# Last transform of a long convolution taken for two token blocks at once, with the MLP's inner units split six and eight

## The chip, the core and the metric

The kernel runs on one core of one Trainium2 chip, as one launch. The metric is the device time of that launch in microseconds; the number quoted for a kernel is the median of its runs. A profiled execution gives the span of the core (first to last recorded instruction), the busy time of each engine, and the waits between engines. The engines are TensorE (PE; its weight loads are listed as PEld), VectorE (DVE), ScalarE (ACT), GpSimd (POOL) and SyncE (SP). In this kernel nearly all DMA transfers are issued by SP, one after the other, in program order.

## The reference

One block of a network with adaptive layer norm: a state-space convolution over 2048 tokens and 448 channels, and behind it an MLP that mixes tokens (not channels), with 1792 inner units.

```python
def _A_ref(u, log_A_real, A_imag, C_real, C_imag, log_dt, D_skip):
    L = u.shape[1]
    ...
    K = 2.0 * jnp.einsum("dn,dnl->dl", C, P).real
    L2 = 2 * L
    u_t = u.transpose(0, 2, 1)
    Kf = jnp.fft.rfft(K, L2)
    Uf = jnp.fft.rfft(u_t, L2)
    y = jnp.fft.irfft(Uf * Kf[None, :, :], L2)[:, :, :L]
    return y.transpose(0, 2, 1) + u * D_skip[None, None, :]

def _B_ref(x, w1, b1, w2, b2):
    h = _layernorm(x, axis=-1)                     # (B, S, D)
    u = jnp.einsum("bsd,sf->bdf", h, w1) + b1      # (B, D, F)
    u = _gelu(u)
    y = jnp.einsum("bdf,fs->bds", u, w2) + b2      # (B, D, S)
    return y.transpose(0, 2, 1)

h = _layernorm(x, axis=-1) * (1 + ca) + sa
x = x + ga * _A_ref(h, ...)
h = _layernorm(x, axis=-1) * (1 + cb) + sb
x = x + gb * _B_ref(h, ...)
```

## The kernel before

**The convolution.** It is a Fourier transform of length 4096 written as small matrix products in two levels (32 by 64). The last level of the inverse transform brings 32 frequencies, each with a real and an imaginary part, back to tokens. Its input is a scratch tensor in device memory, `v_d`, with 32 rows `k` of 128 positions; a position is (part `c` of 2, half `h` of 2, half `g` of 2, row `r` of 16). Token number 64 n + 32 g + 16 h + r is row `r` of halves `g`, `h` and block number n. So the 2048 tokens fall into 16 blocks, one for each `r`, of 128 tokens each.

**From the transform to the MLP.** Each block `r` passes through four stages. `ln_load` reads its 128 x 896 slice `vt` of `v_d`; every other call also reads, with `x_pair`, the input rows `x` of two neighbouring blocks into a tile `xt`. `ln_y` does the transform on TensorE: two products of 128 x 64 weights (`ft`, in which half of the entries are zero, since `h` is kept apart by a block diagonal) into the two halves of the single PSUM tile `y`; then VectorE adds `y` to `xt` with the row sum, and ScalarE takes the square sum. `ln_mod` normalizes and scales, with a second row sum and square sum; `ln_out` normalizes again (the MLP's own layer norm) and splits the block into a rounded part `h3h` and a remainder `h3l`. `mlp1` then multiplies the block with seven 128-column pieces of `w1`: three products a piece (`whi` by `h3h`, `whi` by `h3l`, `wlo` by `h3h`), accumulated in seven PSUM tiles `acc` over all 16 blocks.

**The two passes.** PSUM has eight banks; seven hold `acc`, one holds `y`. So the 1792 inner units are done as two passes of seven 128-unit pieces: the first pass runs together with the transform and the norms, the second reads the finished `h3h`, `h3l` again. Behind each pass `gelu` empties the `acc` tiles. Then the MLP's second layer runs: 16 output blocks `o`, each with 42 products.

**The weights.** `WeightStream` loads `w1` and `w2` through three tiles `w`, 448 KB each; ScalarE rounds `w` to `whi`, VectorE takes the remainder `wlo`. `begin` does the first, `rest` the second and then issues the next load. Four `whi`, `wlo` pairs are kept ahead.

**What sets the order.** The norm phase is a loop of steps t = -3 to 15 whose instructions run on PE, ACT and DVE exactly as written; in step t the program does `ln_out` of block t+1, `ln_y` of block t+3, the load of block t+7, `ln_mod` of block t+2, the weight split, and then `mlp1` of block t. SP's order is also as written from the last loads of the convolution on (`manual_schedule`). `vt` has four buffers, `w` three, `y` one. Ahead of it the convolution's last pieces run: `u` loads, products on VectorE and GpSimd (`zx`, `zy`, `z`), inverse products `vv` on TensorE, copies `vt` on ScalarE and stores to `v_d`. All of `v_d` has to be stored before the first `vt` can be read.

Of the kernel before, what the change touches and what calls it, by code (L numbers as in the profile page):

```python
# [11 lines left out]
F32 = mybir.dt.float32  # L12
# [27 lines left out]
def dft_tables():  # L40
# [75 lines left out]
    ft = np.zeros((32, 2, 2, 32, 2))  # L116
# [32 lines left out]

def token_rows(a):  # L150

    return a.rearrange("(n g h r) d -> r g n h d", g=2, h=2, r=16)


def token_pair(a, r, g):

    rows = a.rearrange("(n g h r) d -> g n h (r d)", g=2, h=2, r=16)
    return rows[g, :, :, r * D : (r + 2) * D]


class WeightStream:
# [12 lines left out]
    def load(self):  # L174
# [3 lines left out]
        w = self.pool.tile([P, 896], F32, tag="w", name="w", bufs=3)  # L178
        if n < 32:
            fh, r = divmod(n, 16)  # L180
            for g in range(2):
                self.nc.sync.dma_start(w[64 * g : 64 * g + 64], self.w1[r, g, :, :, fh * 896 : (fh + 1) * 896])
        else:
            t, kh = divmod(n - 32, 2)
            self.nc.sync.dma_start(
                w.rearrange("p (k s) -> p k s", k=7), self.w2[:, 7 * kh : 7 * kh + 7, t * P : (t + 1) * P]
            )
# [6 lines left out]
    def begin(self, most):  # L194
# [5 lines left out]
        hi = self.pool.tile([P, 896], F32R, tag="whi", name="whi")  # L200
        lo = self.pool.tile([P, 896], F32R, tag="wlo", name="wlo")
# [15 lines left out]
def tile_adaln_s4d_mixer(ctx, tc, i, out):  # L217
# [14 lines left out]
    ft = cp.tile([P, 64], F32, name="ft")  # L232
# [5 lines left out]
    with ExitStack() as es:  # L238
# [894 lines left out]
        py = e3.enter_context(tc.tile_pool(name="py", bufs=1, space=PSUM, side="right"))  # L1133
        xts = [xs.tile([P, 2, D], F32, name=f"xt{r}") for r in range(8)]

        def x_pair(r):
            for g in range(2):
                nc.sync.dma_start(
                    xts[r // 2][64 * g : 64 * g + 64].rearrange("p r d -> p (r d)"), token_pair(x, r, g)
                )  # L1140
# [4 lines left out]
        for m in range(NP, 2 * NP + 2, 2):  # L1145
# [31 lines left out]
    with ExitStack() as es:  # L1177
# [7 lines left out]
        uh = [up.tile([P, 7, D], F32R, name="uh0"), None]  # L1185
        ul = [up.tile([P, 7, D], F32R, name="ul0"), None]
        v_v = v_d.rearrange("k (ch g r) d -> r (k ch) g d", ch=4, g=2)

        def mlp1(acc, n, f0=0, f1=7):
            fh, r = divmod(n, 16)  # L1190
            hi, lo = wst.parts[n]
            if f1 == 7:
# [9 lines left out]
        def ln_load(r):  # L1202
# [161 lines left out]
```

## Time and profile before

| | before |
|---|---|
| median of 3 runs | 719.15 us (715.73 to 719.76) |
| the profiled execution's own time | 720.78 us |
| its span | 719.0 us |
| busy PE, DVE, ACT, POOL | 632.4, 453.2, 438.7, 273.6 us |
| HBM traffic | 84.64 MB read, 34.87 MB written |

The median and the profiled execution differ by 1.63 us, and 1.78 us of the execution lie outside the span. Times in views of the trace count from the span's start. A row of the timeline gives start, duration, engine, line and operation; what stands in brackets is the engine's idle time just before and what ended it. Matmuls are pipelined: one of 448 columns shows a duration of 0.36 us, but in a dense stream the next starts 0.20 us after it, so counts times start distances give the time, not counts times durations. A float32 product (the transform) is shown as two instructions, a rounded one (`fp32r`, the MLP) as one.

### The profile page before, as it was taken

Reading aid. Unit: us, or ns where it says so; the run is one execution under the profiler, and the core shown is the slowest. Engines: PE = TensorE matmul, PEld = TensorE weight load, DVE = VectorE, ACT = ScalarE, POOL = GpSimd, SP = SyncE. Lnnn points to the kernel's source line nnn. Section 1 sums busy time; section 2 is a strip of 40 time slices with the busy share of each in tenths; the row PEclk is TensorE's granted clock in tenths of the full one; section 3 lists DMA queues with packets and bytes.
Section 4 is the critical chain, followed back from the end, with each engine's and each line's share of the span. In section 5 each row is a group of like instructions: output and inputs, shape, how many; then the busy total and the mean of one; then the engine's idle time right before and its main releaser. Section 6 shows DMA issues by size and latency. Waiting matters only on the chain. (4 is left out here: it accounts for less than half of the span.)

```text
span 719.0 us, 18288 instructions
## 1 busy us (share of the span) xinstructions
PE 632.4 (88%) x7204; PEld 456.4 (63%) x7204; DVE 453.2 (63%) x875; ACT 438.7 (61%) x876; POOL 273.6 (38%) x328
## 2 busy tenths in 40 slices
PE   0659889979989888799888949999999999999997
PEld 0335335434535556566565617778999999999996
DVE  7469879679778668586684548778622263334441
ACT  5847588887987789989883549787522242222220
POOL 6486437528737787878785600000000000000000
PEclk9868857988998889999899959999999999999999
DMA  7795464266888635535236989974585436655540
GB/s 169 207 191 131 162 192 138 113 229 179 244 227 248 204 92 133 149 100 154 70 102 181 285 245 266 239 195 113 174 231 146 148 109 172 173 155 154 156 139 26
DMA packets 101635, 121.19 MB, mean 169 GB/s; under 512 B 13066, under 2 KB 87422, under 8 KB 101422
## 3 DMA queue, kind: packets, MB, share of 16 engines
q1 hardware_dynamic: 100014, 113.16, 55.2%
q0 software_dynamic: 1536, 6.87, 4.4%
q8 instruction: 57, 0.93, 0.6%
q14 instruction: 28, 0.23, 0.1%
HBM read 84.64 MB, written 34.87 MB: 166 GB/s over the span
## 5 line engine op out<-in xcount | busy, mean ns | idle before, releaser
L202 ACT CAST whi<-w 128x896 fp32r<-128x896 f32 x64 | 59.7, 938 | 131.4 <-PE o L1331 84.7
L651 POOL TENSOR_TENSOR G<-mag,gs 128x512 f32<-128x512 f32 x56 | 71.9, 1284 | 92.4 <-ACT gs L647 92.1
L211 DVE TENSOR_TENSOR wlo<-w,whi 128x896 fp32r<-128x896 f32 x64 | 68.0, 1087 | 40.3 <-ACT whi L202 31.0
L603 PE MATMUL xg<-tab,lph 64*128 64x512 f32 x112 | 68.8, 617 | 25.9 <-ACT xg L649 8.0
L1196 PE MATMUL acc<-h3h,whi 128*128 128x448 f32 x224 | 83.3, 372 | 0.1
L1197 PE MATMUL acc<-h3l,whi 128*128 128x448 f32 x224 | 81.9, 366 | 0.0
L1331 PE MATMUL o<-ul,whi 128*128 128x448 f32 x224 | 81.3, 363 | 0.0
L1330 PE MATMUL o<-uh,whi 128*128 128x448 f32 x224 | 81.2, 362 | 0.0
L1198 PE MATMUL acc<-h3h,wlo 128*128 128x448 f32 x224 | 80.9, 361 | 0.0
L1332 PE MATMUL o<-uh,wlo 128*128 128x448 f32 x224 | 80.6, 360 | 0.0
L678 PEld LDWEIGHTS kg<-E,G 128*32 128x32 f32 x3584 | 59.8, 119 | 32.3 <-issue 16.4
L603 PE MATMUL xe<-tab,lph 64*128 64x512 f32 x112 | 67.8, 609 | 12.2 <-ACT gs L648 10.2
L678 PE MATMUL kg<-E,G 128*32 128x64 f32 x3584 | 69.8, 235 | 2.2 <-issue 1.5
L652 POOL TENSOR_TENSOR G<-mag,gs 128x512 f32<-128x512 f32 x56 | 71.7, 1280 | 0.0
L653 DVE TENSOR_TENSOR E<-m,xe 128x512 f32<-128x512 f32 x56 | 38.3, 683 | 40.8 <-ACT xe L646 31.8
L632 POOL TENSOR_TENSOR m<-mag,w 128x512 f32<-128x512 f32 x56 | 59.9, 1070 | 6.0 <-DVE E L657 1.5
L1334 DVE SCALAR_TENSOR_TENSOR y<-o,b,mod 128x448 f32<-128x448 f32 x16 | 10.9, 684 | 80.3 <-PE o L1332 80.3
L644 ACT ACTIVATE ab<-xe 128x512 f32<-128x512 f32 x56 | 33.7, 601 | 30.3 <-PE xe L603 16.1
L1196 PEld LDWEIGHTS acc<-h3h,whi 128*128 128x128 f32 x224 | 42.3, 189 | 13.8 <-ACT h L1252 6.3
L603 PE MATMUL xe<-tab,lex 64*128 64x512 f32 x56 | 31.7, 575 | 18.8 <-POOL dsk L468 17.2
L614 ACT ACTIVATE mag<-xe 128x512 f32<-128x512 f32 x56 | 35.5, 634 | 19.7 <-PE xg L603 14.0
L603 PEld LDWEIGHTS xg<-tab,lph 64*128 64x128 f32 x112 | 24.3, 217 | 36.3 <-issue 10.3
(229 smaller groups left out, 1486.1 us busy)
## 6 DMA issues: line engine op xcount, KB each, us to landing
w<-in_B_w_dram SPq DMA_DIRECT2D x64, 224.0 KB
w<-in_B_w_dram SPq DMA_DIRECT2D x32, 448.0 KB
yu_d<-yt SPq DMA_DIRECT2D x16, 448.0 KB
yi<-yu_d SPq DMA_DIRECT2D x32, 224.0 KB
us_d<-uo SPq DMA_DIRECT2D x16, 448.0 KB
u<-us_d SPq DMA_DIRECT2D x32, 224.0 KB
v_d<-vt SPq DMA_DIRECT2D x32, 224.0 KB
vt<-v_d SPq DMA_DIRECT2D x16, 448.0 KB
```

Source lines behind the costliest of these rows:

```text
L211: eng.tensor_tensor(lo, w, hi.bitcast(F32), ALU.subtract)
L603: T.matmul(out[k], lhs[r], rhs[r], start=start, stop=stop)
L632: G.tensor_tensor(m2, me, w[:, :, None].to_broadcast([P, GD, 32]), ALU.mult)
L651: G.tensor_tensor(Gt[:, 1], mg_, v32(sg), ALU.mult)
L652: G.tensor_tensor(Gt[:, 0], mg_, v32(cg_), ALU.mult)
L678: T.matmul(kgs[g][32 * q : 32 * q + 32, m], Gt[:, c, d], E[:, c, d], start=h == 0 and c == 0 and m == 0, stop=h == 1 and c == 1, skip_grou ...
L1196: nc.tensor.matmul(acc[f], hi[:, fs], h3h[:, r], start=r == 0, stop=False)
L1197: nc.tensor.matmul(acc[f], hi[:, fs], h3l[:, r], start=False, stop=False)
L1198: nc.tensor.matmul(acc[f], lo[:, fs], h3h[:, r], start=False, stop=r == 15)
L1330: nc.tensor.matmul(o, hi[:, ks], uh[kh][:, k], start=kh == 0 and k == 0, stop=False)
L1331: nc.tensor.matmul(o, hi[:, ks], ul[kh][:, k], start=False, stop=False)
L1332: nc.tensor.matmul(o, lo[:, ks], uh[kh][:, k], start=False, stop=kh == 1 and k == 6)
```

## The change

The transform takes two blocks at once, `r` and `r + 8`. `ft` becomes 128 x 32: the same 64 x 32 matrix twice, once for each `h`. `vt` is loaded with `h` in the two halves of the partitions (two transfers a block instead of one), so that a block needs four products of 64 x 32 weights, (`h`, `g`), and a pair of blocks eight. Their row half is `h`, and their 32 output columns are `2 g + place`, where `place` is `h` for the first block of a pair and `1 - h` for the second. Thus the eight lie on eight different parts of the array, and the two blocks of a pair write two PSUM tiles `y`.

Two `y` tiles take two banks, so `acc` has six in the first pass, and the 14 pieces of inner units are done as six and eight. The second pass takes the two banks of `y` for its first two pieces. The weight tiles have room for 1024 columns and hold 768 or 1024. The tokens of a block are now stored in four groups of 32 partitions: loads of `w1`, of `x` and the store of the sum are four transfers of 32 partitions where there were two of 64.

The blocks run in the order 0, 8, 1, 9, ...; two tiles of `x` rows are needed from the start, and their loads (`x_pair(0)`, `x_pair(8)`) stand inside the convolution's last pieces. Before, that place had `x_pair(0)` alone, later, and `x_pair(2)` and `x_pair(4)` stood between the first `vt` loads.

```diff
-    ft = np.zeros((32, 2, 2, 32, 2))
+    ft = np.zeros((2, 32, 2, 32))
...
     for h in range(2):
-        ft[:, 0, h, :, h] = f0
-        ft[:, 1, h, :, h] = f1
-    t["FT"] = ft.reshape(P, 64)
+        ft[h, :, 0] = f0
+        ft[h, :, 1] = f1
+    t["FT"] = ft.reshape(P, 32)
...
+def block(b):
+    return 8 * (b % 2) + b // 2
+
+def place(r, c):
+    return c ^ (r >= 8)
+
 def token_rows(a):
-    return a.rearrange("(n g h r) d -> r g n h d", g=2, h=2, r=16)
+    return a.rearrange("(n j r) d -> r j n d", j=4, r=16)
...
+NF = (6, 8)
...
         if n < 32:
             fh, r = divmod(n, 16)
-            for g in range(2):
-                self.nc.sync.dma_start(w[64 * g : 64 * g + 64], self.w1[r, g, :, :, fh * 896 : (fh + 1) * 896])
+            r, cols = block(r), slice(768 * fh, 768 + 1024 * fh)
+            w = w[:, 0 : P * NF[fh]]
+            for c in range(4):
+                self.nc.sync.dma_start(w[32 * c : 32 * c + 32], self.w1[r, place(r, c), :, cols])
...
+            if m == 2 * NP - 6:
+                x_pair(0)
             if m == 2 * NP - 4:
-                x_pair(0)
+                x_pair(8)
...
-        pacc = es.enter_context(tc.tile_pool(name="pacc", bufs=7, space=PSUM))
+        pacc = es.enter_context(tc.tile_pool(name="pacc", bufs=6, space=PSUM))
+        pys.append(e3.enter_context(tc.tile_pool(name="py2", bufs=1, space=PSUM, side="right")))
...
-        v_v = v_d.rearrange("k (ch g r) d -> r (k ch) g d", ch=4, g=2)
+        v_v = v_d.rearrange("k (c h g r) d -> r h k c g d", c=2, h=2, g=2)
...
-        def ln_load(r):
-            vts[r] = rot.tile([P, 2, D], F32, tag="vt", name="vt", bufs=4)
-            nc.sync.dma_start(vts[r], v_v[r])
-            if r % 2 and 1 < r < 15:
-                x_pair(r + 1)
+        def ln_load(b):
+            vts[b] = rot.tile([P, 2, D], F32, tag="vt", name="vt", bufs=4)
+            for h in range(2):
+                nc.sync.dma_start(vts[b][64 * h : 64 * h + 64], v_v[block(b), h])
+            if b > 3 and b % 4 < 2:
+                x_pair(block(b))
...
+        def ln_pair(b):
+            for i in (b, b + 1):
+                ys[i] = pys[i % 2].tile([P, D], F32, tag="y", name="y")
+                vt = vts.pop(i)
+                for h in range(2):
+                    k = slice(64 * h, 64 * h + 64)
+                    for g in range(2):
+                        c = 2 * g + place(block(i), h)
+                        nc.tensor.matmul(ys[i][32 * c : 32 * c + 32], ft[k], vt[k, g], start=True, stop=True)
...
         def ln_y(r):
-            y = py.tile([P, D], F32, tag="y", name="y")
-            vt = vts.pop(r)
-            for g in range(2):
-                nc.tensor.matmul(y[64 * g : 64 * g + 64], ft, vt[:, g], start=True, stop=True)
...
         for r in range(4):
             ln_load(r)
-            if r == 1:
-                x_pair(2)
         wst.load()
...
+            if t in (-3, -1):
+                ln_pair(t + 3)
...
+            if t % 2 and 0 < t < 13:
+                ln_pair(t + 3)
             if t in (-3, -1) or 0 < t < 13:
                 ln_y(t + 3)()
...
         gelu(acc, 0)
-        acc = [pacc.tile([P, D], F32, tag="acc", name="acc") for _ in range(7)]
+        more = es.enter_context(tc.tile_pool(name="more", bufs=2, space=PSUM))
+        acc = [(pacc if f > 1 else more).tile([P, D], F32, tag="acc", name="acc") for f in range(8)]
```

Two places of the order show it. On PE, the rows from the convolution's last inverse products (`vv`) to the first MLP products, before:

```order
L798 MATMUL vv<-z,bt 128x224 x2
L1224 MATMUL y<-vt,ft 64x448 x6
L1196 MATMUL acc<-h3h,whi 128x448
L1197 MATMUL acc<-h3l,whi 128x448
L1198 MATMUL acc<-h3h,wlo 128x448
```

and in the changed kernel:

```order
L815 MATMUL vv<-z,bt 128x224 x2
L1252 MATMUL y<-vt,ft 32x448 x16
L1217 MATMUL acc<-h3h,whi 128x448
L1218 MATMUL acc<-h3l,whi 128x448
L1219 MATMUL acc<-h3h,wlo 128x448
```

Three blocks' transforms of two products each stood ahead of the first MLP product; now four blocks' of four products each do. Later, two transform products stood between one block's 21 MLP products and the next; now eight stand between 36 and 36.

On SP, the last transfers of the convolution (`u` is its last load, `v_d` its stores) and the first of the norm phase, before:

```order
L806 DMA v_d<-vt 128x2x224 x2
L182 DMA w<-in_B_w_dram 64x1x896 x2
L741 DMA u<-us_d 128x448
L806 DMA v_d<-vt 128x2x224 x2
L1138 DMA xt_6073<-in_A_u_dram 64x1x896 x2
L806 DMA v_d<-vt 128x2x224 x4
L1204 DMA vt<-v_d 128x2x448 x2
```

and in the changed kernel:

```order
L823 DMA v_d<-vt 128x2x224 x2
L197 DMA w<-in_B_w_dram 32x768 x4
L1155 DMA xt_6073<-in_A_u_dram 32x896 x4
L758 DMA u<-us_d 128x448
L823 DMA v_d<-vt 128x2x224 x2
L1155 DMA xt_6077<-in_A_u_dram 32x896 x4
L823 DMA v_d<-vt 128x2x224 x4
L1226 DMA vt<-v_d 64x2x448 x8
```

The last `u` load had two transfers between it and the `v_d` stores ahead of it, and now has eight; the first `vt` loads are eight in a row, four blocks' worth.

More of the change, by code (lines that the diff above doesn't have):

```diff
@@ L199, in begin @@
         w = self.raw.pop(n)
[L200 to L201 removed]
+        m = w.shape[-1]
+        hi = self.pool.tile([P, 1024], F32R, tag="whi", name="whi")[:, 0:m]
+        lo = self.pool.tile([P, 1024], F32R, tag="wlo", name="wlo")[:, 0:m]
         self.nc.scalar.copy(hi, w)
```

62 lines of the change are left out of this document (34 added, 28 removed).

## The prediction

> **What bounds the kernel now.** The windows come first: which engine is full, and where. Columns: length of the window, then busy time of PE, PEld, DVE, ACT, POOL with instruction counts, the granted clock, the share of the DMA engines and GB/s.
>
> ```profile
> 395.00:413.00 18.00, 16.70 (x156) 12.28 (x152) 10.83 (x20) 9.17 (x41) 12.39 (x20) 1.00 0.94 284
> 424.00:466.00 42.00, 40.04 (x173) 27.93 (x174) 32.69 (x102) 33.49 (x76) 0.00 (x0) 0.91 1.05 259
> 450.00:492.50 42.50, 42.50 (x202) 32.51 (x201) 32.45 (x98) 33.41 (x72) 0.00 (x0) 1.00 0.81 201
> 512.60:714.00 201.40, 201.40 (x1009) 188.66 (x1007) 77.35 (x99) 48.57 (x55) 0.00 (x0) 1.00 0.52 148
> ```
>
> From 437 us on PE never stops: in the norm phase, and in the 201.4 us of second pass and second layer, 1008 products at 0.20 us each. There only fewer or cheaper PE instructions save time. Next I read one period of the norm phase, from the chain of waits (start, duration, engine, tile):
>
> ```profile
> 457.57 0.90 PE y L1224 x4
> 458.48 0.41 PE acc L1196
> 462.88 0.90 PE y L1224 x4
> ```
>
> The period is 5.31 us. Twenty-one MLP products at 0.20 us are 4.20, so one block's transform costs PE 1.11 us. The same period on DVE and ACT, from the timeline:
>
> ```profile
> 473.17 0.16 DVE L1244 TENSOR_TENSOR mean<-mean,rs 128x1 f32<-128x1 f32 x1
> 474.44 0.62 DVE L1227 SCALAR_TENSOR_TENSOR xt<-xt,y 128x448 f32<-128x448 f32 x1 [1.12 <-PE y L1224]
> 475.30 0.67 ACT L1216 ACTIVATE sq<-xt,mean 128x448 f32<-128x448 f32 x1 [0.56 <-DVE mean L1214]
> 476.87 0.67 ACT L1216 ACTIVATE sq<-h,mean 128x448 f32<-128x448 f32 x1 [0.48 <-DVE mean L1214]
> 477.28 1.08 DVE L211 TENSOR_TENSOR wlo<-w,whi 128x896 fp32r<-128x896 f32 x1
> 477.86 0.93 ACT L202 CAST whi<-w 128x896 fp32r<-128x896 f32 x1
> ```
>
> DVE waits 1.12 us a period for `y` and nothing else, ACT 0.56 + 0.48 for DVE. So DVE needs 5.31 - 1.12 = 4.19 us a block and ACT 4.27: the reserve under PE is only about 1 us. Last the entrance to the phase, where PE is idle, from the timeline and (the row of `v_d` without a line) the chain of waits:
>
> ```profile
> 404.79 0.95 SPq L806 DMA_DIRECT2D v_d<-vt  x2
> 405.79 1.18 SPq L182 DMA_DIRECT2D w<-in_B_w_dram  x2
> 407.07 0.53 SPq L741 DMA_DIRECT2D u<-us_d  x1
> 411.23 0.62 DVE L781 TENSOR_TENSOR zx<-kx,u 128x448 f32<-128x448 f32 x1 [1.91 <-DMA u<-us_d]
> 415.23 2.07 DMA v_d<-vt
> 417.48 1.23 SPq L1204 DMA_DIRECT2D vt<-v_d  x2
> 421.52 1.76 PE L1224 MATMUL y<-vt,ft 128*64 128x448 f32 x4 [6.99 <-DMA vt<-v_d]
> 423.33 0.62 DVE L1227 SCALAR_TENSOR_TENSOR xt<-xt,y 128x448 f32<-128x448 f32 x1 [3.66 <-PE y L1224]
> 434.13 0.17 DVE L1243 RECIPROCAL rs<-rs 128x1 f32<-128x1 f32 x1 [1.16 <-ACT rs L1217]
> 436.70 0.62 DVE L1254 TENSOR_TENSOR h3l<-h,h3h 128x448 fp32r<-128x448 f32 x1
> 437.07 0.47 PE L1196 MATMUL acc<-h3h,whi 128*128 128x448 f32 x1
> 441.35 0.62 DVE L1254 TENSOR_TENSOR h3l<-h,h3h 128x448 fp32r<-128x448 f32 x1
> 512.46 0.36 PE L1196 MATMUL acc<-h3h,whi 128*128 128x448 f32 x1
> ```
>
> This is one chain: the last `u` load, the last piece of the convolution, its store, the first `vt`, then DVE and ACT in turn up to the remainder `h3l` of block 1 (437.3), when block 1's MLP products begin (437.07). What makes `u` or `vt` late there shifts all that follows. The last row is the start of the second pass (the first pass's last product begins 0.2 us before): 75.4 us after 437.07.
>
> **The change, part by part. The transform of a pair.** What does it cost PE? Rows of the transform, of a full-array float32 product of the same length, and of 64 x 64 products on four parts of the array (line views: least/median/largest ns; timeline):
>
> ```profile
> L1224 PE MATMUL y<-vt,ft x64: 539/590/1009, 421.5 to 495.1; 128*64 128x448 f32 x64
> L557 PE MATMUL pu<-yi,s x64: 539/539/1114, 165.5 to 231.9; 128*128 128x448 f32 x64
> 457.50 0.97 PE L1224 MATMUL y<-vt,ft 128*64 128x448 f32 x4
> 381.75 1.16 PE L716 MATMUL y<-wc,ks 64*64 64x64 f32 x62 [0.22 <-ACT vt L804]
> ```
>
> An instruction takes 0.54 us at any width, yet four of the transform are through in 0.97: the two column halves run side by side, and only the two instructions of one half follow each other. With eight parts the same 0.97 holds for a pair, plus the issue of 12 more instructions. L716 issues 62 in 1.16 us, 0.019 each: 0.23 us. Pair: 1.11 + 0.23 = 1.34 us instead of 2.22. Bounds: 1.11 (issue hidden) and 2.22 (only four parts at once). I take 1.34, since L716 is the nearest row with both row and column parts. The Trainium skill, "TensorE: Matmul & The Clock Gate", section "Measured speedup vs the span model", gives about 4 ns for each further tile; by it the pair would cost about 1.16 us and the sum below would be 0.9 us lower. L716's 19 ns, for short products, does not agree with that figure.
>
> **The first pass.** From block 1's products to the second pass: before, 15 blocks x 21 x 0.20 = 63.0 and eleven transforms x 1.11 = 12.2, together 75.2 (75.4 measured). After, 15 x 18 x 0.20 = 54.0 and five pairs x 1.34 = 6.7: 60.7. **-14.7 us.** The sixth pair lies ahead of block 1's products, as the first did, in a wait for `h3l`.
>
> **The second pass** gets eight pieces: 16 x 3 x 0.20 = **+9.6 us** on a full PE. The two passes and layers hold the same 1344 products; the three of block 0 that leave the first pass save nothing, as PE waits there anyway. At the change of passes PE has no gap today, so the two extra banks win nothing; `gelu` of the second pass's eight pieces lies beside the first six pieces of the second layer (3.6 us).
>
> **DVE and ACT.** Their weight splits shrink by 128/896 in the first pass, 0.14 and 0.13 us: 4.05 and 4.14 us a block, against PE's (36 x 0.20 + 1.34)/2 = 4.27. PE stays the bound by 0.13 us, but not at the start: `h3l` of block 2 ends at 441.97 today, 4.9 us after block 1's products begin, and PE, with 3.6 us of work, is there 0.8 us early (its first product of block 2 does not need `h3l`). **+0.8 us**; between 0.4 and 1.2, and nothing more later, as from block 3 on the pairs put PE behind again.
>
> **SP's queue.** Rows of issue cost:
>
> ```profile
> L182 SPq DMA_DIRECT2D w<-in_B_w_dram x64: 528/578/1782, 382.4 to 552.9; - x64
> L1204 SPq DMA_DIRECT2D vt<-v_d x16: 562/563/613, 417.5 to 479.7; - x16
> L741 SPq DMA_DIRECT2D u<-us_d x32: 319/334/1531, 240.7 to 407.1; - x32
> L589 SPq DMA_DIRECT2D lph<-pars x27: 302/381/2071, 27.2 to 344.2; - x27
> 398.02 0.88 SPq L806 DMA_DIRECT2D v_d<-vt  x2
> ```
>
> Two blocks issue 8 `w`, 4 `vt` and on average 4 `x` transfers, where 4, 2 and 2 stood. Transfers of plain rows (L741, L589, L806) take 0.32 to 0.38, with the gap 0.44 to 0.46; today's `w`, whose 64 partitions are gathered with two strides, 0.58. The new `w` and `x` are plain rows of 32 partitions like L589: 0.45 each; `vt` I leave at 0.56 + 0.06. Four steps: 16 x 0.45 + 8 x 0.62 + 8 x 0.45 = 15.8 us in 17.1 us of PE time. It fits; `w` is issued three steps ahead of its use and `vt` about four. In the second pass, 8 x 0.45 = 3.6 in 4.8. Bytes: two blocks move 0.92 + 0.79 + 0.46 = 2.17 MB in 8.54 us, 254 GB/s, under the 259 and 284 of the first two rows.
>
> **The entrance.** Behind the `v_d` stores at 404.79 the last `u` now waits for eight transfers of 0.45 (3.6 us) where two took 1.3: issued 2.3 us later. It landed 4.0 us after its issue with 0.46 MB just ahead of it; the eight move 0.85 MB, but spread over 3.6 us (236 GB/s, no backlog), so it may land up to 1.2 us sooner after issue. DVE waits for it today, hence 1.1 to 2.3 us of delay: **+1.7**. Then the first pair needs two blocks of `vt`, not one: 0.46 MB more at 284 GB/s is 1.6 us, at least 0.6 (one issue later), at most 2.2 with the issue of 16 instructions at the low clock (0.91 in the window): **+1.6**. That `x` is no longer between them is in this.
>
> **Sum:** -14.7 + 9.6 + 0.8 + 1.7 + 1.6 = -1.0 us against the execution's 720.78 (span 719.0 and 1.78 around it), which lies 1.6 above the median; on the median, 719.15 - 1.0 = **718.1 us**.
>
> **The rivals. Row halves get in each other's way (slower).** The two row halves of a block now write one PSUM tile. No row of before shows that: L716, L603 and L798, which use row halves, write each half to a tile of its own. If two row halves could not write one bank at once, a pair would go in three stages (half 0 of block 1; half 1 with half 0 of block 2; half 1 of that), each further one two instructions of 0.97 - 0.54 = 0.43: 1.11 + 4 x 0.43 = 2.8 us. Five pairs x 1.5 = 7.3: 725.4. It decides from a pair of about 2 us on. For it: the halves were kept apart so far. Against: the columns differ, so no partition of the bank gets two results. The Trainium skill says it flatly: "Different row tiles cannot access same PSUM bank simultaneously" ("TensorEngine Tiling (Array Packing)", "Gotcha 1: PSUM Pressure"); by that rule this rival is the result, and no run here shows it yet.
>
> **SP becomes the queue that sets the pace (slower).** If 32-partition transfers cost 0.58 with 0.05 around them, as `w` today, four steps need 16 x 0.63 + 8 x 0.62 + 8 x 0.63 = 20.1 us against 17.1. Two such groups give 6 us of lag, of which three steps of lead cover some 3; the entrance gets another 1.4 (8 x 0.18). 718.1 + 3 + 1.4 = 722.5. For it: every 64-partition load is dear; against: L589.
>
> **The entrance costs nothing (faster).** If `u` lands as early as before and the two `vt` together, as no `x` stands between them, the 3.3 us vanish; with a pair at 1.11 another 1.2: 713.6. For it: in the first window the DMA engines carried 284 GB/s; against: DVE's wait of 1.91 us on `u`.
>
> **How the numbers follow.** Chances: forecast 0.52, row halves 0.12, SP 0.16, free entrance 0.20. The forecast's own bounds: low, -1.0 - 1.2 (pair) - 1.6 (entrance) - 0.4 = -4.2, 714.9; high, the late ends of `u`, `vt` and `h3l` (0.6 + 0.6 + 0.4) with a pair at 2.22 (+4.4), 724.1, though a pair near 2 is unlikely. Range with the rivals: 713.8 to 723.5, which leaves out the row-half rival and the lowest tail. A measurement of this kernel can tell about 0.5%, 3.6 us, from no change: faster means below 715.6, slower above 722.7. Faster: 0.16 of the free entrance and 0.12 of the forecast, 0.28; slower: 0.12, 0.08 of SP and 0.07 of the forecast's upper end, 0.27; within: 0.45.
>
> **What would show it.** One transform row of 16 instructions about 1.2 us long, every 8.5 us; 36 products between; PE full from block 3 on. If the row is 2 us or more, the array parts do not all run together. If DVE's wait for `y` is gone and PE waits for `h3l` in each step, DVE or ACT has become the bound. The last `zx` some 1.7 us later than 411.2 and the first transform some 3 us later than 421.5 show the entrance. SP rows of 0.58 for `w` would show the queue. The prediction is wrong if the second pass starts before 497 or after 506 us, or if gaps show in the second pass.

## The result, and the profile after

The changed kernel takes 720.28 us (median of 20 runs, 716.89 to 724.37); the kernel before, run beside it, 716.36 us (20 runs, 710.65 to 721.21). The ratio is 1.0068, with a 95% interval of 1.0047 to 1.0088: slower, by 3.4 to 6.3 us, where I forecast 1.0 us less. (The kernel before had 719.15 us from three executions when I forecast; from 20 it is 2.8 us less, so ratios and not medians are compared below.) The profiled execution of the changed kernel takes 720.45 us, its span is 718.5.

The two profiled executions differ by 5.3 us before the change begins: the same row of the chain of waits (16 products `kx`) starts at 384.07 us before and at 378.81 after. That is scatter of the part ahead of it: in the 18 other executions below the row starts between 373.8 and 384.7 us, whatever the edit. So I measure distances from that row. The chain of waits of the changed kernel, from there to the first MLP product:

```profile
378.81 1.76 PE kx L789 x16
...
404.29 3.48 DMA u<-us_d
407.90 0.63 DVE zx L798
...
414.94 3.43 DMA vt<-v_d
418.41 2.72 PE y L1252 x8
...
427.27 0.74 PE acc L1217
```

The entrance (`kx` to the first MLP product) is 427.27 - 378.81 = 48.46 us; before it was 45.42 (384.07 to 429.49). The last `u` comes late, as forecast: its product `zx` starts 29.09 us after `kx`, before 27.16. The first transform starts 39.60 us after `kx` (418.41), before 37.45 (421.52 in the prediction's lines), so 2.15 of the 3.0 us are there when it starts and the other 0.9 come between it and the first MLP product. Block 1's first product, the first of the second pass and the last of all, from PE's timeline of the changed kernel and then, the last alone, of the kernel before (its two others are in the prediction):

```profile
435.28 0.47 PE L1217 MATMUL acc<-h3h,whi 128*128 128x448 f32 x1
...
500.07 0.36 PE L1217 MATMUL acc<-h3h,whi 128*128 128x448 f32 x1
...
713.42 0.36 PE L1370 MATMUL o<-uh,wlo 128*128 128x448 f32 x1
```

```profile
713.87 0.36 PE L1332 MATMUL o<-uh,wlo 128*128 128x448 f32 x1
```

| stretch, us | before | after | difference | forecast |
|---|---|---|---|---|
| entrance: `kx` to first product of block 0 | 45.42 | 48.46 | +3.0 | +3.3 |
| first pass: block 0 to second pass | 82.97 | 72.80 | -10.2 | -13.9 |
| second pass and second layer, to the last product's start | 201.41 | 213.35 | +11.9 | +9.6 |
| `kx` to the last product | 329.80 | 334.61 | +4.8 | -1.0 |

So 3.7 us are missing in the first pass and 2.3 behind it. In the second pass PE has no gap, but its 1056 products start 213.35 / 1055 = 0.2022 us apart; before, 1008 products started 201.41 / 1007 = 0.2000 apart. In the first pass PE waits at the pairs. The rows of PE's weight loads at the first instruction held up in each pair (in brackets the idle time and what ended it):

```profile
444.33 0.14 PEld L1252 LDWEIGHTS y<-vt,ft 64*32 64x32 f32 x4 [0.73 <-DMA vt<-v_d]
453.09 0.14 PEld L1252 LDWEIGHTS y<-vt,ft 64*32 64x32 f32 x4 [0.24 <-DMA vt<-v_d]
462.87 0.14 PEld L1252 LDWEIGHTS y<-vt,ft 64*32 64x32 f32 x4 [1.26 <-DMA vt<-v_d]
471.56 0.14 PEld L1252 LDWEIGHTS y<-vt,ft 64*32 64x32 f32 x4 [0.16 <-DMA vt<-v_d]
480.89 0.14 PEld L1252 LDWEIGHTS y<-vt,ft 64*32 64x32 f32 x4 [0.81 <-DMA vt<-v_d]
```

Each time it is the second block's `vt` that is late, 3.2 us in all. Why it is late can be read from two views. SP's timeline over four steps of the first pass (start, duration, number of transfers):

```profile
442.60 1.23 SPq L1226 DMA_DIRECT2D vt<-v_d  x2
443.87 1.99 SPq L1155 DMA_DIRECT2D xt<-in_A_u_dram  x4
445.97 2.07 SPq L197 DMA_DIRECT2D w<-in_B_w_dram  x4
...
458.28 3.09 SPq L197 DMA_DIRECT2D w<-in_B_w_dram  x4
461.47 1.23 SPq L1226 DMA_DIRECT2D vt<-v_d  x2
```

SP issues almost without a pause, and four steps take it 461.47 - 442.60 = 18.9 us. A transfer of `w` or `x` mostly takes it 0.42 us and 0.04 to the next, one of `vt` 0.59; about 2 of the 18.9 us are short waits and what one `w` issue of 1.59 us (in the row of 3.09) has over the others. So the issues alone need about 17 us, and PE, undisturbed, 16.8 (run e16 below). And the windows, of the kernel before and then of the changed one (columns as in the prediction):

```profile
420.00:440.00 20.00, 15.80 (x55) 8.44 (x56) 11.97 (x42) 11.31 (x27) 0.00 (x0) 0.71 1.05 283
440.00:460.00 20.00, 20.00 (x96) 15.08 (x95) 16.63 (x49) 17.57 (x40) 0.00 (x0) 1.00 1.04 253
460.00:480.00 20.00, 20.00 (x96) 15.08 (x95) 15.02 (x44) 16.03 (x36) 0.00 (x0) 1.00 0.89 216
```

```profile
420.00:440.00 20.00, 19.11 (x84) 9.49 (x79) 14.13 (x47) 13.45 (x33) 0.00 (x0) 0.74 1.06 237
440.00:460.00 20.00, 20.00 (x115) 15.82 (x115) 18.45 (x58) 18.70 (x43) 0.00 (x0) 1.00 0.98 237
460.00:480.00 20.00, 19.54 (x118) 15.13 (x122) 17.00 (x53) 17.38 (x43) 0.00 (x0) 1.00 1.01 232
```

The DMA share stays at 1.0 for 60 us, at 232 to 237 GB/s (shares over 1 come from packets that overlap in time: up to 20 are in flight at once between 440 and 480 us). Before, it fell to 0.89 from 460 us on: the loads had got ahead. PE's busy time (20.00, then 19.54 of 20) hardly shows the waits at the pairs; the start distances of its products do.

### The profile page after: what moved, and what is told of

It is laid out like the page before. It is cut to its first block, busy times and chain, and to the rows that moved or that the text cites. A ratio compares the mean times of both kernels' runs of the same rounds, so it can differ in the third digit from the quotient of the medians.

```text
span 718.5 us, 18589 instructions
## 1 busy us (share of the span) xinstructions
PE 632.9 (88%) x7268; PEld 456.3 (64%) x7268; DVE 454.4 (63%) x875; ACT 437.8 (61%) x876; POOL 273.1 (38%) x328
## 5 line engine op out<-in xcount | busy, mean ns | idle before, releaser
L219 ACT CAST whi<-w 128x768 fp32r<-128x768 f32 (+1 forms) x64 | 59.7, 938 | 140.9 <-PE o L1369 85.1
L228 DVE TENSOR_TENSOR wlo<-w,whi 128x768 fp32r<-128x768 f32 (+1 forms) x64 | 68.0, 1086 | 48.1 <-ACT whi L219 33.5
L695 PEld LDWEIGHTS kg<-E,G 128*32 128x32 f32 x3584 | 59.0, 119 | 30.4 <-issue 15.8
L661 ACT ACTIVATE ab<-xe 128x512 f32<-128x512 f32 x56 | 33.8, 603 | 29.2 <-PE xe L620 18.2
L631 ACT ACTIVATE mag<-xe 128x512 f32<-128x512 f32 x56 | 35.6, 635 | 17.6 <-PE xg L620 11.9
```

The source lines that it names most:

```text
L228: eng.tensor_tensor(lo, w, hi.bitcast(F32), ALU.subtract)
L695: T.matmul(kgs[g][32 * q : 32 * q + 32, m], Gt[:, c, d], E[:, c, d], start=h == 0 and c == 0 and m == 0, stop=h == 1 and c == 1, skip_grou ...
```

## The experiments

Distances are those of the table: entrance, first pass, second pass to the last product, and their sum. They come from one execution of each run. e1 leaves the order of the entrance as it is, and its entrance is 0.76 us shorter than that of the changed kernel, so differences of less than about 1 us in the entrance or the first pass show little.

| run | median us | ratio to before, 95% interval | entrance | first pass | second | sum |
|---|---|---|---|---|---|---|
| after | 720.28 | 1.0068 (1.0047 to 1.0088) | 48.46 | 72.80 | 213.35 | 334.61 |
| e1 | 718.4 | 1.0054 (1.0022 to 1.0086) | 47.70 | 73.37 | 211.00 | 332.07 |
| e2 | 719.15 | 1.0039 (1.0012 to 1.0065) | 45.00 | 83.72 | 203.63 | 332.35 |
| e3 | 715.53 | 1.0006 (0.9978 to 1.0034) | 45.29 | 83.20 | 201.40 | 329.89 |
| e4 | 771.68 | 1.0799 (1.0764 to 1.0833) | 53.43 | 114.14 | 218.19 | 385.76 |
| e5 | 721.57 | 1.0073 (1.0049 to 1.0098) | 48.91 | 73.36 | 213.34 | 335.61 |
| e6 | 719.52 | 1.0045 (1.0016 to 1.0074) | 47.51 | 73.91 | 213.34 | 334.76 |
| e7 | 717.36 | 1.0017 (0.9994 to 1.0040) | 47.57 | 72.64 | 210.99 | 331.20 |
| e8 | 721.88 | 1.0086 (1.0052 to 1.0120) | 45.37 | 84.32 | 205.88 | 335.57 |
| e9 | 720.23 | 1.0078 (1.0046 to 1.0110) | 53.19 | 68.95 | 213.34 | 335.48 |
| e10 | 718.11 | 1.0033 (1.0000 to 1.0066) | 48.69 | 71.38 | 213.34 | 333.41 |
| e11 | 721.01 | 1.0059 (1.0028 to 1.0090) | 53.41 | 70.04 | 211.00 | 334.45 |
| e12 | 715.98 | 1.0009 (0.9980 to 1.0039) | 45.40 | 74.04 | 211.00 | 330.44 |
| e13 | 723.52 | 1.0106 (1.0089 to 1.0123) | 48.41 | 76.89 | 213.34 | 338.64 |
| e16 | 716.43 | 1.0002 (0.9981 to 1.0024) | 47.98 | 69.00 | 213.34 | 330.32 |
| e17 | 723.0 | 1.0090 (1.0059 to 1.0121) | 47.65 | 75.96 | 211.00 | 334.61 |
| e18 | 721.73 | 1.0074 (1.0045 to 1.0104) | 50.71 | 69.94 | 213.34 | 333.99 |
| e19 | 719.06 | 1.0043 (1.0021 to 1.0065) | 51.71 | 71.30 | 211.00 | 334.01 |
| e20 | 717.04 | 1.0029 (1.0003 to 1.0055) | 48.68 | 73.48 | 210.99 | 333.15 |

### The products: e1, e2, e3, e8

In the memory layout of the compiled programs `h3h`, `h3l`, `uh`, `ul` (the moving operands of all MLP products) begin 32 bytes above a multiple of 256 before, and 160 above after: `ft`, which lies ahead of them, shrank from 256 to 128 bytes a partition. The weight tiles' pitch also changed, from 3584 to 4096 bytes. e1 gives the changed kernel `ft`'s old room, e2 shifts the kernel before by 128 bytes, e3 gives it the new pitch (`w`, `whi` and `wlo` alike), e8 shifts it to a multiple of 256.

```diff
e1 (after)   -    ft = cp.tile([P, 32], F32, name="ft")
             +    ft = cp.tile([P, 64], F32, name="ft")[:, 0:32]
e2 (before)  -    ft = cp.tile([P, 64], F32, name="ft")
             +    ft = cp.tile([P, 96], F32, name="ft")[:, 0:64]
e8 (before)  +    ft = cp.tile([P, 120], F32, name="ft")[:, 0:64]
e3 (before)  -        w = self.pool.tile([P, 896], F32, tag="w", name="w", bufs=3)
             +        w = self.pool.tile([P, 1024], F32, tag="w", name="w", bufs=3)[:, 0:896]
```

> The changed kernel with the transform's weight tile ft given room for 64 columns again (only 32 used), so that every tile behind it, h3h, h3l, uh and ul among them, starts at the byte address it has in the kernel before (32 instead of 160 above a multiple of 256). Address theory (MLP products are 2.2 ns slower because their moving operand starts elsewhere): three MLP products take 0.600 us instead of 0.607, 1344 products win 2.9 us, ratio to before about 1.003. Pitch theory (the 1024-column weight tiles do it) and run theory (it is the chip or the run): three products stay at 0.607, ratio 1.007.

> The kernel before with 128 more bytes behind ft, so that h3h, h3l, uh and ul start at 160 above a multiple of 256, as in the changed kernel, and nothing else moves. Address theory: three MLP products take 0.607 us instead of 0.600, 2.9 us more in all, ratio 1.004. Pitch theory and run theory: 0.600 and ratio 1.000.

> The kernel before with weight tiles w, whi, wlo of 1024 columns of which 896 are used: their addresses are those of the changed kernel, the operands h3h, uh stay where they were. Pitch theory: three MLP products take 0.607 us, ratio 1.004. Address theory and run theory: 0.600, ratio 1.000.

> The kernel before with 224 bytes of empty room behind `ft`, so that `h3h`, `h3l`, `uh`, `ul` start at a multiple of 256 bytes (before: 32 above one, product 0.2000 us; shifted by 128: 0.2022); nothing is left out. Theory 'the start within 256 bytes of the moving operand counts, and a start on the boundary is best': a product takes 0.2000 us or less, the median is that of before or lower. Rival 'it is the place relative to something else (the weights' tiles, which stay where they are)': the product takes between 0.2000 and 0.2022 us or more, and the median is 0 to 3 us above.

Rows of the groups of instructions (busy us, mean ns of one), of the kernel before, of e2, of e8, and then of e1 and the changed kernel:

```profile
L1332 PE MATMUL o<-uh,wlo 128*128 128x448 f32 x224 | 80.6, 360 | 0.0
```

```profile
L1332 PE MATMUL o<-uh,wlo 128*128 128x448 f32 x224 | 82.3, 367 | 0.0
L1330 PE MATMUL o<-uh,whi 128*128 128x448 f32 x224 | 80.9, 361 | 0.0
```

```profile
L1332 PE MATMUL o<-uh,wlo 128*128 128x448 f32 x224 | 82.3, 368 | 0.0
L1330 PE MATMUL o<-uh,whi 128*128 128x448 f32 x224 | 82.2, 367 | 0.0
```

```profile
L1369 PE MATMUL o<-ul,whi 128*128 128x448 f32 x224 | 80.6, 360 | 0.0
```

```profile
L1369 PE MATMUL o<-ul,whi 128*128 128x448 f32 x224 | 82.4, 368 | 0.0
```

One of the three products of a triple is 7 ns longer in e2 than in the kernel before, in e8 two are (`uh` by `whi` has 362 in the kernel before). The start distances, as a mean over the three, say the same: 0.2000 us in e1 (211.00 / 1055) and e3, 0.2022 in e2 (203.63 / 1007), 0.2044 in e8 (205.88 / 1007). (e2's profiled execution was the slowest of its eleven, 724.0 us; the median of e1, at a ratio of 1.0054, can't tell the theories apart, its distances can.) So the move of the tiles behind `ft`, the moving operands among them, is shown to be the cause in both directions, 2.3 us behind the first pass and 288 x 0.0022 = 0.6 in it; the pitch is not. My rule for it fell in e8: a multiple of 256 is the worst of the three starts, not the best. Nor does the start of an operand decide by itself: in e2 `uh` is slow with `wlo` and not with `whi`, and in the changed kernel, with the same 160 bytes, `ul` with `whi` is the slow one. What the start is to be compared with (the weights' tiles stayed where they were in e1, e2 and e8) is open.

### What one part does: e12

The kernel before with the split in six and eight alone (`NF = (6, 8)`, six `acc` tiles, 1024-column weight tiles); transform, token rows and transfers as before.

> The kernel before with only the inner units in six and eight blocks (transform, token rows and transfers as before); nothing left out. It moves 48 products (9.6 us) from the first pass to the second. Theory 'the first pass of the kernel before has room in its transfers': its stretch from block 0 to the second pass falls by 9.6 from 83.0 to 73.4 us, the second pass grows by as much, the median is that of before (ratio 1.000). Rival 'the first pass is near the transfers' limit even before the change' (253 to 263 GB/s at a share of 1.04 from 430 to 460 us): the stretch falls to 75 to 77 us only, and the median is 2 to 4 us above before.

PE's timeline of e12 at the start of block 0 and of the second pass, and its windows:

```profile
423.19 0.74 PE L1203 MATMUL acc<-h3h,whi 128*128 128x448 f32 x1
...
497.23 0.36 PE L1203 MATMUL acc<-h3h,whi 128*128 128x448 f32 x1
```

```profile
440.00:460.00 20.00, 20.00 (x94) 14.80 (x93) 16.95 (x54) 18.00 (x40) 0.00 (x0) 1.00 0.99 241
460.00:480.00 20.00, 20.00 (x96) 15.06 (x95) 16.79 (x52) 17.40 (x40) 0.00 (x0) 1.00 0.79 188
```

The first pass falls by 8.9 of 9.6 us and the time is that of before: the split costs nothing that these runs can tell. Yet e1, which has the pairs as well and its products at the same 0.2000, has a first pass of 73.37 against 74.04 here: the pairs, each worth 1.1 us on PE (next section), bring 0.7 us in all, no more than the scatter, and the entrance that they need costs 2.3.

### What the pairs cost, and what they wait for: e16, e5, e6, e7

e16 leaves out the weight loads of blocks 5 to 12; their products use block 4's weights.

```diff
+        if 5 <= n < 13:
+            self.raw[n] = self.last
+            self.loaded += 1
+            return
```

> The changed kernel without the weight loads of blocks 5 to 12 (the products use block 4's weights again, so the output is wrong for them): 32 transfers and 3.1 MB less in the first pass. Both theories expect the waits at the pairs to be gone and the stretch from block 0 to the second pass to be 68 to 69 us (products 58.2, seven pairs 9.4, and 1 us of waits for the first halves), with the entrance unchanged; the median about 716. If the stretch stays above 71, something on PE, ACT or DVE sets the pace and not the transfers.

The first products of blocks 5, 7, 9 and 11 in e16, from PE's timeline:

```profile
448.12 0.47 PE L1221 MATMUL acc<-h3h,whi 128*128 128x448 f32 x1
...
456.51 0.47 PE L1221 MATMUL acc<-h3h,whi 128*128 128x448 f32 x1
...
464.91 0.47 PE L1221 MATMUL acc<-h3h,whi 128*128 128x448 f32 x1
...
473.30 0.47 PE L1221 MATMUL acc<-h3h,whi 128*128 128x448 f32 x1
```

Two blocks take 8.39 us (16.8 for the four steps of SP's row above); 36 products of 0.2022 are 7.28, so an undisturbed pair costs PE 1.11 us, the lower of my bounds, and ACT and DVE keep up. With the loads gone the first pass is 69.0 us. That the transfers hold it is shown; which limit of theirs, not yet, since e16 takes away issues and bytes at once.

e5 issues both `vt` of a pair together and the `x` loads in the other steps; e6 issues the first four `x` blocks behind the last `u`; e7 is both with e1's room.

```diff
e5  -            if 4 <= t + 7 < 16:
    +            if t % 2 and 4 <= t + 7 < 16:
                     ln_load(t + 7)
    +                ln_load(t + 8)
    +            if t in (-2, 2, 6):
    +                x_pair(block(t + 6))
    +                x_pair(block(t + 7))
e6  -            if m == 2 * NP - 6:
    +            if m == 2 * NP - 4:
                     x_pair(0)
    -            if m == 2 * NP - 4:
    +            if m == 2 * NP - 2:
                     x_pair(8)
```

> The changed kernel with both `vt` loads of a pair issued together at odd steps and both `x` loads at even steps; nothing is left out. Theory 'late by place in the queue': SP issues the second block's `vt` a step after the first's, behind eight other transfers, so issuing it earlier ends the waits of PE at the pairs (0.73, 0.24, 1.26, 0.16, 0.81 us, 3.2 in all) down to under 0.5 us; the way from the product of block 1 to the second pass falls from 64.7 to about 61.7 us and the median from 720.3 to about 717.2. Rival 'the transfers fill the DMA engines' (share 0.98 and 1.01 from 440 to 480 us): the same bytes must land before the same products, so the wait turns up at `w` or `x` (ACT's `whi` waits, or DVE's residual), the way stays at 64 to 65 us and the median at 720.

> The changed kernel with the loads of the first four `x` blocks issued one step later, behind the last `u`; nothing is left out. Theory 'the last `u` waits in SP's queue': SP issues it about 2 us sooner, the wait of the product by the kernel's spectrum for it falls from 3.86 to about 2 us, the way from `kx` to the first MLP product falls from 48.5 to about 46.6 us, and the median from 720.3 to about 718.4. Rival 'given back': the `x` blocks then land after the first transforms, the first residual waits for them, the way stays at 48 us or more and the median at 720.

> The changed kernel with all three: `ft`'s old place, `vt` loads together, first `x` loads later. By my theories the three terms add (2.9 for the products, 3.2 for the `vt` waits, 1.9 for the entrance): 720.3 - 8.0 = 712.3 us, ratio to the kernel before about 0.994. If the DMA engines' share is what sets the first pass, only the products' and at best the entrance's terms come: 715.5 to 717.5, ratio about 1.000.

The order alone gives nothing. In e5 the waits for `vt` shrink, and PE waits as long for a remainder instead (the last two numbers of the group's row are its idle time before and that by its releaser):

```profile
L1218 PE MATMUL acc<-h3l,whi 128*128 128x448 f32 x224 | 83.0, 370 | 3.4 <-DVE h3l L1286 3.4
```

e6 enters 0.95 us sooner, little more than the scatter, and gives it back in the first pass. e7 keeps the products' term and a part of the entrance's; it is, beside e20, the best version with pairs that leaves nothing out, and does not beat the kernel before.

### SP's issue or the DMA engines: e9, e10, e11, e13, e18, e20

e10 halves the bytes of `x` (for blocks 4 to 15 only one row of each pair is loaded, the other is set to zero) with as many transfers. e9 issues `x` on POOL's queue; e11 is e7 with `x` of blocks 4 to 11 loaded earlier, among the convolution's last loads; e13 is e9 with each load held back by a copy on POOL that waits for an earlier block. e18 issues `w` of blocks 3 to 15 on POOL's queue, held to their steps by the three `w` buffers; e20 is the same from block 5 on, with e1's room.

```diff
e10 -                x_pair(block(b))
    +                for c in range(4):
    +                    nc.sync.dma_start(xts[r // 2][32 * c : 32 * c + 32, 0], token_pair(x, r, c)[:, 0:D])
e9  -                x_pair(block(b))
    +                x_pair(block(b), G)
e13 +                G.tensor_copy(rot.tile([P, 1], F32, tag="gate", name="gate"), gate)
    +                x_pair(block(b), G)
e11 +            if m in (NP + 2, NP + 4):
    +                x_pair(m - NP)
    +                x_pair(m - NP + 8)
e18 +            eng = self.nc.gpsimd if 3 <= n < 16 else self.nc.sync
    -                self.nc.sync.dma_start(w[32 * c : 32 * c + 32], self.w1[r, place(r, c), :, cols])
    +                eng.dma_start(w[32 * c : 32 * c + 32], self.w1[r, place(r, c), :, cols])
```

> The changed kernel with the `x` loads of blocks 4 to 15 issued on POOL's queue (POOL is idle there) in place of SP's; the same bytes, nothing left out. SP loses 24 of its transfers in the first pass. From the first product of block 0 to the second pass the changed kernel takes 72.8 us, of which 288 products of 0.2022 and seven pairs of 1.34 are 67.6: 5.2 us are waits. Theory 'SP's issue sets the pace': SP saves 4 us in each four steps (18.9 to 15), the pairs no longer wait for `vt`, the stretch falls to 68 to 69.5 us and the median from 720.3 to about 716.5. Rival 'the DMA engines are full' (they moved 234 GB/s at a share of 1.0 in the changed kernel): the stretch stays at 72 to 74 us, the median at 720.

> The changed kernel in which the `x` transfers of blocks 4 to 15 move only the first row of each pair, the other row being zeros, so the output is that of another input; the number of transfers is the same, 1.38 MB of the some 17 MB of the first pass is gone. Theory 'the DMA engines are full': 1.38 MB at 234 GB/s is 5.9 us, all of it between steps -3 and 7, where the pairs wait; the stretch from block 0 to the second pass falls from 72.8 to 68 to 70 us, the median from 720.3 to about 716.5. Theory 'SP's issue sets the pace': as many issues, at most 10% shorter each; the stretch stays at 72 or more, the median at 720.

> Run e7 (padding, `vt` loads together, first `x` loads later) in which the `x` rows of blocks 4 to 11 are loaded about 30 us earlier, among the last loads of the convolution, where the DMA share was 0.6 to 0.9; nothing left out. SP loses 16 transfers and the engines 1.8 MB in the first pass, so both theories expect the waits of the first pass (72.6 us in e7, 67.0 of them products and pairs) to fall to 1 to 2 us. If nothing is given back ahead of it: 717.4 - 4 = 713.4 us, ratio to the kernel before 0.996. Rival 'given back': the entrance waits for `u` or `v_d` by 2 to 4 us more, and the median stays at 717.

> The changed kernel with the `x` loads of blocks 4 to 15 on POOL's queue, each behind a small copy on POOL that waits for the first residual or for `h3h` of eight blocks earlier, so that they start in the same steps as in the changed kernel; the same bytes at the same time, nothing left out. Theory 'SP's issue sets the pace of the first pass': the entrance stays at 48 to 49 us, the stretch from block 0 to the second pass falls from 72.8 to 69 to 70 us, the distance from `kx` to the last product from 334.6 to about 331.3, the median from 720.3 to about 717. Rival 'the DMA engines are full': the stretch stays at 72 to 73 and the median at 720.

> The changed kernel with the first pass's weight loads of blocks 3 to 15 on POOL's queue; three `w` buffers hold each of them back to its own step, so nothing moves into the entrance (where e9, e11 and e13 moved `x`); the same bytes, nothing left out. SP loses 16 of the 32 transfers of four steps. Theory 'SP's issue sets the pace of the first pass after its first blocks': the stretch from block 0 to the second pass falls from 72.8 to 69 to 70 us (69.0 with the loads of eight blocks gone, e16), entrance 48 to 49, the median from 720.3 to 716.5 to 717.5. Rival 'the DMA engines are full': 72 us or more, median 720.

> e19 with the weights of blocks 3 and 4 back on SP's queue, behind the `vt` loads, since in e18 and e19 POOL issued them 5 us sooner, into the entrance, and the first product came 2.3 us later. Nothing left out. If the engines have room once the entrance is past: entrance 47.7 to 48.5, first pass 69 to 70.5, second pass to the end 211.0, `kx` to the last product 328 to 330, the median 714.5 to 716.5, ratio to the kernel before 0.998 to 1.001. If the engines are full from the entrance to block 8, so that entrance and first pass together stay at 120 to 121 whatever queue issues: 331 to 332.5, median 717.5 to 718.5.

**Bytes less, issues as many (e10).** Two windows and two rows of SP's timeline of e10:

```profile
440.00:460.00 20.00, 20.00 (x116) 16.08 (x116) 18.75 (x59) 18.97 (x44) 0.00 (x0) 1.00 0.88 220
460.00:480.00 20.00, 20.00 (x115) 15.76 (x115) 17.37 (x56) 17.79 (x40) 0.00 (x0) 1.00 0.73 185
```

```profile
442.86 1.23 SPq L1226 DMA_DIRECT2D vt<-v_d  x2
...
461.09 1.23 SPq L1226 DMA_DIRECT2D vt<-v_d  x2
```

The engines have room (0.88, 0.73), but four steps still take SP 18.2 us, without a pause (one issue of 1.32 us in it), and the first pass gains only 1.4 us. Neither theory had that figure: what is left to hold the pass here is, as far as these views show, SP.

**Issues less, bytes as many (e18, e20).** Windows of e18, then of e20:

```profile
440.00:460.00 20.00, 20.00 (x119) 16.23 (x117) 17.23 (x53) 17.09 (x41) 7.94 (x17) 1.00 1.06 232
460.00:480.00 20.00, 19.14 (x113) 14.83 (x112) 17.49 (x53) 16.80 (x40) 7.84 (x17) 1.00 1.06 249
```

```profile
440.00:460.00 20.00, 19.28 (x110) 14.74 (x110) 17.15 (x53) 16.71 (x39) 8.88 (x19) 1.00 1.06 234
```

Now the engines are full for longer. e18's first pass falls to 69.9 us as the theory of SP's issue had it, but two weight loads ran ahead into the entrance, which grew by 2.3 us; entrance and first pass together stay at 120.7 (121.3 in the changed kernel). e20 held these two back, and there its rival was nearer: 48.7 + 73.5 = 122.2 us, against 120 to 121 in the rival. Measured against e1, which has the same room for `ft` (121.1), it gains nothing, although SP now pauses for up to 2.0 us at a time. e9, e11 and e13 are of this kind as well: each moved `x` ahead, and the entrance, or block 0 in e13 (13.65 us to block 1, with 4.75 of PE waiting for `vt`), grew by as much or more: 122.1, 123.5 and 125.3.

So there are two limits close to each other: SP's issue, 17 us for four steps and 18 to 19 with its waits, and the engines. Taking one away leaves the other; only e16, which took issues and bytes, let the pairs pay (117.0). e17 (e13 with e6's order and e1's room) and e19 (e18 with e1's room) were meant as best versions:

> e13 with `ft`'s old place and the first four `x` blocks loaded behind the last `u`; nothing left out. If the terms add: entrance 46.7 to 47.5, first pass 69 to 70, second pass to the end 211.0, so `kx` to the last product 327 to 328.5 (before 329.8): the median 713.5 to 715.5, ratio to the kernel before 0.996 to 0.998. If the DMA engines are full: first pass 72 to 73, 717.4 as in e7.

> The same with `ft`'s old place, so that the products take 0.2000 us. If both terms come: entrance 47.7 to 48.5, first pass 68.5 to 69.5, second pass to the end 211.0: `kx` to the last product 327.5 to 329 (329.8 before), the median 713.5 to 715.5, ratio to the kernel before 0.996 to 0.999. If the engines are full: 718.4 as in e1.

They took 723.0 us and 719.06 us, and miss in the way of e13 and e18: in e17 the first pass grew to 75.96 us, in e19 the entrance to 51.71 (together 123.6 and 123.0).

### Fewer and larger transfers: e4

One transfer of 128 partitions in place of four, for `w1` and `x` of the blocks with r < 8, whose token groups stand in natural order.

```diff
+            if r < 8:
+                self.nc.sync.dma_start(w, self.w1[r, :, :, cols])
-            for c in range(4):
+            for c in range(4 if r >= 8 else 0):
```

> The changed kernel with one transfer of 128 partitions instead of four of 32 for w1 and x wherever the block's row is below 8 (the rows from 8 on keep four, their groups being swapped). Same bytes. Over four steps SP issues 10 w and 5 x transfers instead of 16 and 8. Queue theory (SP's issue time makes vt late): SP is no longer busy without a break between 440 and 476 us, PE's waits for vt at the pairs (3.2 us) fall below 1 us, and at the entrance u is issued 1.2 us earlier: together 4 us less than the changed kernel, ratio about 1.001. Bandwidth theory (the DMA engines are full, share about 1.0): the waits stay, only the entrance gains about 1.2 us, ratio about 1.005.

It took 771.68 us (ratio 1.0799, 1.0764 to 1.0833), which neither theory had. Its waits (total us, times, longest) and one window:

```profile
ACT whi L221 <- DMA w<-in_B_w_dram: 109.7, 24, 9.4
```

```profile
440.00:460.00 20.00, 12.71 (x54) 8.32 (x56) 8.42 (x25) 8.10 (x20) 0.00 (x0) 0.83 0.61 132
```

The weights come late while the engines' mean share is only 0.61. The Trainium skill, "DMA: Bandwidth & Descriptors", section "Why a DMA increments its semaphore by 16 and not by 1", has a rule that would do this: a transfer is spread over the largest number of engines, up to 16, that divides the slowest dimension of both sides. Here the source's slowest dimension is the four token groups, so four engines would carry it; the 32-partition transfers have 32 there. The low share agrees. No row names an engine, but the start and end of every DMA packet are in the trace: from 440 to 540 us of e4 exactly four packets (of 512 bytes or more) are in flight for 36% of the time, and 15 or more for 32%; in the changed kernel from 440 to 480 us it is four for 0.5% and 15 or more for 84%. That four engines carry such a transfer is not shown by name, but it is what these counts look like.

## Why the prediction was wrong, step by step

The 720.28 us lie inside the range that I gave, 713.8 to 723.5, but that owes much to luck: the errors (2.9 and 3.9 us upward, 1.2 downward) cancel in part and still turn the sign of the change, and the base was 2.8 us too high. My sign of being wrong did not fire either: counted from the `kx` of before, the second pass starts at 384.07 + 121.26 = 505.3 us, within 497 to 506, and products that are 2.2 ns longer leave no gap.

**Products at 0.20 us each: the size that failed.** I took 0.20 us for every MLP product of the changed kernel, as "fewer or cheaper PE instructions" were to be the only thing that counts in the second pass. They take 0.2022, since the smaller `ft` moved their operands: 2.3 us behind the first pass and 0.6 in it. e1 and e2 show this. Nothing in the trace of before spoke of it.

**"Bytes: ... 254 GB/s, under the 259 and 284 of the first two rows", and "It fits": the step that failed.** I needed 2.17 MB for two blocks in 8.54 us and compared with the highest rates that I had quoted. The changed kernel's engines carry 232 to 237 GB/s at a share of 1.0 in this phase: 2.17 MB at 234 are 9.3 us for two blocks, and from block 3 to block 11 two blocks took 9.14. The row with 259 GB/s had already shown a share of 1.05, and that with 284 one of 0.94, so those rates were what nearly full engines gave with another mix of transfers, not room. What I had put at nothing, PE's wait for `vt`, cost 3.9 us in five pairs. The chance of 0.16 for SP was the nearest rival. Its condition did not come true: an issue of `w` takes 0.42 us, with the gap 0.46, as forecast, not 0.58. But four steps took 18.9 us against 15.8 forecast, since the first of four `x` takes 0.6, and since waits and one long issue make `w` 0.59 on average from start to start. Whether the smaller transfers lower the engines' rate by themselves was not tried alone; e12, with 64-partition transfers, moved 241 GB/s at 0.99, and e18, with `w` on POOL's queue, up to 249 at 1.06.

**The pair: right in kind, too dear in size.** 1.34 us forecast, 1.11 in e16. The rival of the row halves fell: two row halves write one bank, and a pair takes no longer than one block's transform did. The Trainium skill's sentence that would forbid it ("TensorEngine Tiling (Array Packing)", "Gotcha 1: PSUM Pressure") does not hold for this case, where they write different partitions of the bank. The estimate by the Trainium skill's 4 ns a tile ("TensorE: Matmul & The Clock Gate", "Measured speedup vs the span model"), 1.16, was nearer than mine by L716.

**Right:** the entrance in sum (+3.0 against +3.3), with the last `u` late as said (+1.9 against +1.7); the term of the first `vt` came to 1.1 against 1.6, and only 0.2 of it lies ahead of the first transform. Also right: the move of 48 products to the second pass (e12), no gap at the change of passes, PE as the bound ahead of DVE and ACT once the loads are there (e16).

The sum: -1.0 forecast, +2.3 and +0.6 for the products, -0.3 in the entrance, +3.9 for the waits for `vt`, +0.4 between blocks 0 and 1 (8.01 us against 7.58), -1.2 for five pairs 0.23 cheaper than forecast, -0.1 for the first `h3l` (0.7 in e16: 5.30 us from block 2 to block 3, 4.64 in the later pairs): +4.6 of the +4.8 measured. The waits are 3.2 us in the rows shown, but each pair that is held up loses 0.12 to 0.15 us more than its row has: from block 4 to block 5, for example, 5.02 us, in e16 4.64, with 0.24 in the row. Between blocks 0 and 1 the pair waits for `vt` as well (0.75 us in PE's weight loads, at a low clock); what the 0.4 is made of was not traced further.

## What to carry to other kernels

When a change takes work off the bound engine in a stretch, divide the bytes of the stretch by the rate at which its DMA engines stand at a share of 1.0 with the same kind of transfers, and count the issuing queue as well. Here two blocks needed 8.4 us of PE, 9.3 of the DMA engines and 8.5 of SP; with times that close, shortening the engine's work moves the wait and no more. A change of any small tile can move all tiles behind it; compare the start distances of untouched instructions before looking for a cause in the changed ones.

## What the hardware showed that I had not expected

Where the moving operands start changes the mean rate of the products: 0.2000, 0.2022 and 0.2044 us for a 128 x 128 product of 448 columns with operands at 32, 160 and 0 bytes above a multiple of 256, the weights unmoved; one or two products of each three carry all of it. Eight float32 products of 64 x 32 weights on eight parts of the array, two PSUM banks with two row halves each, cost PE 1.11 us, as much as two of 128 x 64 before. One 128-partition transfer in four groups of 32 came later than four transfers of the groups, and took the engines' mean share from 1.0 to 0.6, with exactly four packets in flight for a third of the time.
